# First group of a fused lightning-attention and tanh-shrink kernel: whole scores, other load order, first unit by token halves

## The chip, the cores and the metric

The kernel runs on one core of one Trainium2 chip. The metric is the device time of one execution in microseconds (us); a time without a profile is the median of several runs.

## The reference

Two parts are computed, one after the other, in 32-bit floating point.

```python
# attention: q, k, v are (4 batches, 8 heads, 768 positions, 64); one decay lam per head
for b in range(nb):                      # blocks of 64 positions, in order
    intra = einsum(qb, kb) * Dmask       # Dmask[i, j] = lam ** (i - j) for i >= j, else 0
    intra = einsum(intra, vb)
    inter = einsum(qb * lam_pow, kv_state)
    out[:, :, sl] = intra + inter
    kv_state = lam_block * kv_state + einsum(kb * rev_pow, vb)
# bridge: x is (3072 tokens, 512), the heads side by side
h = x @ w_in                             # w_in (512, 2048)
y = (h - tanh(h)) @ w_out                # w_out (2048, 512)
```

The result does not depend on the length of a block; the kernel takes blocks of 128 positions.

## The kernel before, in words

The kernel works through six **groups**. A group is one block of 128 positions in all four batches, 512 tokens. Only the very beginning concerns us here: group 0, whose attention starts from an empty state, and the first **unit** of its first matrix product. A unit is 512 of the 2048 hidden columns; there are four, 0 to 3.

**Loads.** `load_natural(g, b, names)` loads q, k or v of one batch, 256 KB each, in runs of 256 bytes. In group 0 the loads are spread over the queues of three engines: SP, ACT and POOL (GpSimd). k and v come in three DMAs: four heads whole, and the other four with the two halves of the positions exchanged. `load_weights` and `load_block` load a block of w_in (128 rows of one unit, 512 KB, in runs of 2 KB, because the input is 64 bits wide) into one of four buffers `raw64`. Block 0 goes over POOL's queue, blocks 1 to 15 over SP's. `ready["may"]` limits how many blocks may be loaded. A dictionary `begin` makes the next DMA of an engine wait for a given instruction; `tied` and `keep_in_program_order` fix the order of instructions on an engine.

**Rounding.** `weights(n)` turns loaded blocks into usable weights with `round_block`: three ScalarE (ACT) instructions (L320 to L322) and two VectorE (DVE) instructions (L324, L325).

**Attention of one batch ("chunk").** `att_transpose`: eight TensorE (PE) transposes, four of q and four of k, each four copied by ACT (L369). `att_scores`: 16 products in six pieces of 64 positions (L387, L389), then two DVE products with a `mask` of decays (L393). `att_decay`: k times its decay, one DVE instruction (L399). `kv_products`: the new state of two batches (L408), copied by `att_state` (L415). `att_out`: the outputs of two batches, in a part over all keys for the later queries (L462) and a part over half the keys (L473), then two ACT copies into `xt` (L484). The profile shows every 32-bit product as two records; a transpose is one.

**The mask.** Eight DVE scans (L110) make the decays into `whole`; a copy and a sum (L113, L114) make the six-piece `mask` of it.

**First unit.** `up_plain(0, order)` yields after each of its 16 steps. A step (i, c) is one block i of w_in times one of four outputs: c = 11 and 21 are the two halves of the unit's columns for the tokens of batches 0 and 1, c = 12 and 22 for batches 2 and 3. Every step is two products (L847), and each output is finished by tanh (L852) and a DVE difference (L853). `idle_products(n)` are n products nobody reads (L344).

The order on PE in group 0 is written out by hand: chunk 0 and chunk 1 up to the scores; the state of batches 0, 1; the transposes of chunk 2; the outputs of batches 0, 1; scores 2; transposes 3; one step of unit 0; scores 3; one step; state and outputs of batches 2, 3; then the 14 other steps. The steps take blocks 0 and 1 for all tokens first and blocks 2 and 3 after that.

Behind unit 0 come units 1 to 3 in the same way, with group 1's attention between them (`powers` is called once among them, before group 1 first needs decays), and then the second product and the other groups.

Of the kernel before, what the change touches and what calls it, by code (L numbers as in the profile page):

```python
# [18 lines left out]
BLK = 128  # L19
# [5 lines left out]
def kernel(  # L25
# [81 lines left out]
    for j in range(2):  # L107
        for p in range(NP):
            h = 2 * p + j
            nc.vector.tensor_tensor_scan(out=whole[:, j, p, :], data0=lam_all[:, h:h + 1].to_broadcast([128, BLK]),  # L110
                                         data1=ident if p < 2 else wide[:, HALF:HALF + BLK], initial=0.0, op0=AL.mult,
                                         op1=AL.add)
    nc.vector.tensor_copy(mask[:, :, 2:6, :], whole[:, :, :, HALF:BLK])  # L113
    nc.vector.tensor_tensor(mask[:, :, 0:2, :], whole[:, :, 0:2, 0:HALF], whole[:, :, 2:4, 0:HALF], op=AL.add)  # L114
# [12 lines left out]
    bwd = mask.rearrange("s j p i -> s p j i")[:, 2:6, :, HALF - 1:HALF].to_broadcast([128, NP, 2, D])  # L127

    def tied(yes, op):
        return tc.keep_in_program_order(op) if yes else op  # L130
# [12 lines left out]
    def load_natural(g, b, names):  # L143
        for name, src, bufs in (("q", q, 2), ("k", k, 3), ("v", v, 4)):
            if name in names:
                if (g, b, name) in ((0, 2, "q"), (0, 3, "q"), (0, 3, "k")):
                    x = opool.tile([128, H, D], F32, name=f"{name}_nat", tag="o")
                else:
                    x = (qpool if name == "q" else io).tile([128, H, D], F32, name=f"{name}_nat", tag=name, bufs=bufs)
                rows = src[b, :, ts(g, BLK), :].rearrange("h s d -> s h d")  # L150
                if name == "q":
                    parts = [(nc.sync, x, rows)]
                else:
                    eng = nc.sync if g > 0 else nc.scalar if b == 0 else nc.gpsimd
                    whole_ = {(0, 1, "k"): nc.scalar, (0, 2, "k"): nc.gpsimd}.get((g, b, name), nc.sync)
                    parts = [(eng, x[ts(1 - t, HALF), 4:8], rows[ts(t, HALF), 4:8]) for t in range(2)]
                    parts.insert(2 * (whole_ is nc.gpsimd), (whole_, x[:, 0:4], rows[:, 0:4]))
# [72 lines left out]
    def load_block(eng, dst, kind, n, m, first=False):  # L230

        if kind == "out":
            tied(first, eng.dma_start(out=dst, in_=moe_w_out[ts(m * KH + n, 128), :].rearrange("k (a n) -> k a n", a=2)))
        elif m < 2:
            op = tied(first, eng.dma_start(out=dst, in_=w_in_u[ts(m, 128), :, ts(n, 256)]))
            if begin.get(eng) is not None:
                wait_for(op, begin.pop(eng))
        else:
            for j in range(2):
                tied(first, eng.dma_start(out=dst[ts(1 - j, 64)], in_=w_in_u[ts(2 * m + j, 64), :, ts(n, 256)]))  # L240

    def load_weights(n):

        while ready["loaded"] < min(n, ready["may"]):
            if moe_w_in.dtype != F32:
                raw64 = stage.tile([128, 2, 256], I64, name="raw64", tag="raw64", bufs=WAHEAD)
                block = blocks[ready["loaded"]]
                load_block(nc.gpsimd if ready["loaded"] in (0, *range(NU * KI, NU * KI + 4)) else nc.sync, raw64, *block, True)
                wraw[ready["loaded"]] = raw64
            ready["loaded"] += 1  # L250

    def weights(n):

        while ready["done"] < min(n, len(blocks)):
            at_ = ready["done"]
            load_weights(at_ + WAHEAD)
            kind, n_, m = blocks[at_]
            if kind == "out" and m == 0:
                pair[n_] = pair_tiles(n_)
            w = w1[n_][:, m] if kind == "in" else pair[n_][m][:, 0:2]  # L260
            if at_ in wraw:
                round_block(w, wraw.pop(at_), at_ < 2 * KI)
            else:
                load_block(nc.gpsimd, w, kind, n_, m)
            ready["done"] += 1
# [110 lines left out]
    def att_scores(g, bs):  # L376
        for b in bs:
            qt, kt, _ = tr[g, b]

            sp = [bank("sp", "att", 4)[:, 0:6 * HALF].rearrange("s (x i) -> s x i", x=6) for _ in range(2)]  # L380
            for p in (0, 2, 1, 3):
# [14 lines left out]

    def att_decay(g, b):
        kp = raw[g, b]["k"].rearrange("s (p j) d -> s p j d", j=2)
        return tied(g != 1, nc.vector.tensor_tensor(kp, kp, bwd, op=AL.mult))  # L399

    def kv_products(g, bs):

        kv = bank("kv", *(("yb", 1) if g >= GB else ("att", 4))).rearrange("d (b p e) -> d b p e", b=2, p=NP)
# [9 lines left out]
    def att_state(g, bs):  # L413
        kv = kv_products(g, bs)
        tied(True, nc.scalar.activation(state[:, bs[0]:bs[0] + 2], kv, AF.Copy))  # L415

    reads = {}
# [24 lines left out]
    def att_out(g, bs):  # L442
# [15 lines left out]
        for n, b in enumerate(bs):  # L458
            ss, vn = sc[g, b], raw[g, b]["v"]
            for p in range(NP):  # L460
                for j in range(2):
                    tied(g == 0, nc.tensor.matmul(out=dst(n, p, j)[:, HALF:BLK], lhsT=vn[:, 2 * p + j, :],  # L462
                                                  rhs=ss[:, j, 2 + p, :], start=g == 0 and n == 0 and p % 2 == 0,
                                                  stop=n == 1 and p % 2 == 1, skip_group_check=True))
        if g < GB:
            kv = kv_products(g, bs) if g > 0 else None
# [443 lines left out]
            next(it)  # L910


    for b in (0, 1):
        att_transpose(0, (b,))
        idle_products(2 + b)
        op = att_decay(0, b)
        att_scores(0, (b,))
        if b == 0:
            idle_products(2)
    begin.update({nc.sync: op, nc.gpsimd: op})  # L920
    for b, names in ((3, "qk"), (2, "v"), (3, "v")):
        load_natural(0, b, names)
    att_state(0, (0, 1))
    att_transpose(0, (2,))

    def one_more(op):
        begin[nc.sync] = op
        ready["may"] = ready["loaded"] + 1
        load_weights(len(blocks))

    one_more(att_out(0, (0, 1)))
    unit = up_plain(0, [(2 * n + i, c + 10 * a) for n in range(KI // 2) for c in (11, 12) for i in range(2) for a in range(2)])
    att_decay(0, 2)
    att_scores(0, (2,))
    weights(1)
    idle_products(2)
    att_transpose(0, (3,))
    idle_products(5)
    one_more(att_decay(0, 3))
    steps(unit, 1)  # L940
    one_more(att_scores(0, (3,)))
    ready["may"] = len(blocks)
    steps(unit, 1)
    weights(2)
    att_state(0, (2, 3))
    att_out(0, (2, 3))
    idle_products(2)
    weights(3)
    steps(unit, 6)
    weights(4)  # L950
    steps(unit, 4)
    weights(6)
    every(unit)
    weights(2 * KI)
# [177 lines left out]
```

## Time and profile before

| | us |
|---|---|
| median of 3 runs | 655.33 (653.83 to 655.36) |
| the profiled execution | 656.1 |
| its span, first to last instruction | 654.3 |
| PE busy in the span | 646.3 (99%) |
| DVE / ACT / POOL busy | 468.9 / 244.0 / 208.8 |
| mean granted TensorE clock | 0.997 |

The span is 1.8 us shorter than the profiled execution's own time, and that execution took 0.8 us more than the median. Views are told in us from the start of the span. In the lines of the profile, "PEld" is the load of PE's weights, an "x32" counts records, and `out<-in` names what is written and read.

### The profile page before, as it was taken

Reading aid. Unit: us, or ns where it says so; the run is one execution under the profiler, and the core shown is the slowest. Engines: PE = TensorE matmul, PEld = TensorE weight load, DVE = VectorE, ACT = ScalarE, POOL = GpSimd, SP = SyncE. Lnnn points to the kernel's source line nnn. Section 1 sums busy time; section 2 is a strip of 40 time slices with the busy share of each in tenths; the row PEclk is TensorE's granted clock in tenths of the full one; section 3 lists DMA queues with packets and bytes.
Section 4 is the critical chain, followed back from the end, with each engine's and each line's share of the span. In section 5 each row is a group of like instructions: output and inputs, shape, how many; then the busy total and the mean of one; then the engine's idle time right before and its main releaser. Section 6 shows DMA issues by size and latency. Waiting matters only on the chain.

```text
span 654.3 us, 15111 instructions
## 1 busy us (share of the span) xinstructions
PE 646.3 (99%) x5888; PEld 593.3 (91%) x5888; DVE 468.9 (72%) x889; ACT 244.0 (37%) x485; POOL 208.8 (32%) x362
## 2 busy tenths in 40 slices
PE   8899999999999999999999999999999999999998
PEld 7788888888888999988999988999988899998897
DVE  4357888968878895678786668788468687466663
ACT  3676865622321222532223442213453213263210
POOL 6000135766133335202335302243401164410241
PEclk9899999999999999999999999999999999999999
DMA  9759976997769768957657956476967476721374
GB/s 196 192 168 199 260 236 216 386 276 211 172 135 224 226 183 253 212 103 184 199 178 222 246 123 167 139 241 203 232 130 160 111 265 222 223 66 35 87 246 165
DMA packets 156951, 125.80 MB, mean 192 GB/s; under 512 B 127744, under 2 KB 130048, under 8 KB 156880
## 3 DMA queue, kind: packets, MB, share of 16 engines
q0 software_dynamic: 27168, 87.91, 43.2%
q1 hardware_dynamic: 128096, 36.53, 26.4%
q8 instruction: 47, 0.77, 0.5%
q10 hardware_dynamic: 1616, 0.39, 0.4%
q14 instruction: 24, 0.20, 0.1%
HBM read 103.81 MB, written 20.97 MB: 191 GB/s over the span
## 4 chain that ended last, share of the span: by engine, by line
PE 93%; DVE 3%; DMA 2%; ACT 1%; issue 1%; ACTq 0%; DVEq 0%
PE y L553 17%; PE y L791 13%; PE zw L791 10%; PE h L847 8%; PE y L637 7%; PE z L553 6%; PE w L738 5%; PE y L738 5%; PE acc L877 4%; PE z L637 3%; PE op L462 2%; PE sp L387 2%; PE w L637 2%; PE kv L408 1%; PE op L433 1%; PE op L473 1%
## 5 line engine op out<-in xcount | busy, mean ns | idle before, releaser
L696 POOL DMA_DIRECT2D wb<-fine x148 | 79.7, 539 | 186.0 <-PE y L738 68.4
L795 ACT ACTIVATE q<-y 128x128 f32<-128x128 f32 x96 | 26.6, 277 | 142.3 <-PE y L791 141.4
L791 PE MATMUL y<-wb,g 128*128 128x128 f32 x456 | 60.2, 277 | 0.0
L847 PE MATMUL h<-xt,w 128*128 128x256 f32 x256 | 57.8, 382 | 0.4 <-DVE w L325 0.4
L791 PEld LDWEIGHTS y<-wb,g 128*128 128x128 f32 x456 | 55.1, 192 | 0.6
L847 PEld LDWEIGHTS h<-xt,w 128*128 128x128 f32 x256 | 47.6, 190 | 7.8 <-DVE w L325 1.0
L699 POOL DMA_DIRECT2D wb<-factors x44 | 23.7, 541 | 83.1 <-PE y L738 50.8
L561 ACT ACTIVATE th<-g 128x512 f32<-128x512 f32 x40 | 25.2, 630 | 66.5 <-DVE g L579 50.7
L553 PE MATMUL y<-xt,w 128*128 128x256 f32 x192 | 45.0, 379 | 0.0
L562 DVE TENSOR_TENSOR g<-g,th 128x512 f32<-128x512 f32 x40 | 27.6, 690 | 20.7 <-ACT th L561 20.7
L553 PEld LDWEIGHTS y<-xt,w 128*128 128x128 f32 x192 | 36.4, 190 | 5.1 <-ACT g L570 0.2
L791 PE MATMUL zw<-wb,g 128*128 128x128 f32 x304 | 40.3, 275 | 0.0
L393 DVE TENSOR_TENSOR ss<-sp,mask 128x384 f32<-128x384 f32 x48 | 23.7, 549 | 20.4 <-PE sp L389 20.4
L553 PE MATMUL y<-tt,ws 128*128 128x256 f32 x160 | 37.8, 379 | 0.0
L553 PE MATMUL y<-tt,w 128*128 128x256 f32 x160 | 37.8, 379 | 0.0
L553 PE MATMUL z<-xt,ws 128*128 128x256 f32 x160 | 37.8, 379 | 0.0
L738 PE MATMUL y<-wb,g 128*128 128x256 f32 x160 | 37.3, 379 | 0.0
L791 PEld LDWEIGHTS zw<-wb,g 128*128 128x128 f32 x304 | 37.0, 192 | 0.2 <-DVE g L797 0.2
L738 PE MATMUL w<-wb,g 128*128 128x256 f32 x160 | 35.3, 379 | 0.0
L553 PEld LDWEIGHTS z<-xt,ws 128*128 128x128 f32 x160 | 30.4, 190 | 4.1
L738 PEld LDWEIGHTS w<-wb,g 128*128 128x128 f32 x160 | 30.4, 190 | 4.1
L738 PEld LDWEIGHTS y<-wb,g 128*128 128x128 f32 x160 | 30.4, 190 | 4.1
(206 smaller groups left out, 1475.0 us busy)
## 6 DMA issues: line engine op xcount, KB each, us to landing
wb<-fine POOLq DMA_DIRECT2D x148, 256.0 KB, 3.5
wb<-factors POOLq DMA_DIRECT2D x44, 256.0 KB, 4.4
wb<-fine_in POOLq DMA_DIRECT2D x36, 256.0 KB, 4.1
raw<-in_moe_w_out_dram SPq DMA_DIRECT2D x12, 512.0 KB, 5.9
rest<-fine POOLq DMA_DIRECT2D x20, 256.0 KB, 4.8
raw<-in_moe_w_in_dram SPq DMA_DIRECT2D x16, 256.0 KB, 6.3
fine<-f POOLq DMA_DIRECT2D x16, 256.0 KB, 5.1
q_blk<-in_q_dram SPq DMA_DIRECT2D x128, 32.0 KB, 2.8
```

The lines of the kernel that those rows point to most:

```text
L393: op = tied(g != 1, nc.vector.tensor_tensor(ss[:, j], sp[j], mask[:, j], op=AL.mult))
L553: nc.tensor.matmul(out=t[:, m, :], lhsT=wt[:, kt, ts(m, 128)], rhs=x[:, kt, :], start=first and m == 0 and kt == 0, stop=kt == 1, skip_gro ...
L561: nc.scalar.activation(th, src, AF.Tanh)
L562: nc.vector.tensor_tensor(dst(c), src, th, op=AL.subtract)
L637: nc.tensor.matmul(out=dst[:, ts(u, 128)], lhsT=a, rhs=b, start=x in (1, 2, 5) and u == 0, stop=True, skip_group_check=True)
L696: nc.gpsimd.dma_start(out=t.rearrange("p m c -> p (m c)"), in_=fine[TWICE.index(n_), SUB.index(x_)].rearrange("p u c -> p (u c)"))
L699: nc.gpsimd.dma_start(out=t, in_=factors[XAT[FACT[n_][1]]][:, 2 * x_:2 * x_ + 2, :])
L738: nc.tensor.matmul(out=t[:, m, :], lhsT=a[:, u, kt, ts(m, 128)], rhs=wb[:, kt, :], start=first and u == 0 and m == 0 and kt == 0, stop=u = ...
L791: tied(x == STEPS[-1], nc.tensor.matmul(out=dst, lhsT=a[:, u, :], rhs=wb[:, ts(u, 128)], start=x in (1, 2) and u == 0, stop=u == NU - 1, s ...
L795: nc.scalar.activation(keep, dst, AF.Copy)
L847: tied(u == 0, nc.tensor.matmul(out=hm[c][:, m, :], lhsT=w1[u][:, i, a, ts(m, 128)], rhs=xt[0, t][:, i, :], start=m == 0 and i == 0, stop= ...
L877: nc.tensor.matmul(out=acc[n][:, r, :], lhsT=a[:, ts(r, 128)], rhs=b, start=kt == 0 and r == 0, stop=kt == KH - 1, skip_group_check=True)
```

## The change

All of it lies in group 0 and unit 0, but for one piece of DVE work that is moved into `powers`.

- k and v of group 0 come in one DMA each, positions in order: k of batches 0 and 1 on ACT's queue, the other k and all v on POOL's. Scores of group 0 are eight whole products of 128 keys by 128 queries per chunk, multiplied by `whole`; outputs are eight whole products (`first_out`, `first_tokens`).
- All w_in blocks go over SP's queue. Blocks 0 and 1 are asked for right behind q of batch 1; q2 and k2 are held until the scores of chunk 0 are multiplied, block 2 until those of chunk 1 are, and q3, k3, v2, block 3 and v3 until the first copy of the tokens of batches 0 and 1.
- The outputs of batches 0 and 1 no longer wait for chunk 2: chunks 0 and 1 are finished first, then two steps of unit 0 follow, and the parts of chunks 2 and 3 stand between further pairs of steps. The steps run by token halves: all four blocks for batches 0, 1, then all four for batches 2, 3.
- The states are copied later; kv of batches 0, 1 waits in another PSUM bank.
- The scans all use `ident`; four scans and the two instructions of `mask` (and a copy) are made in `masks`, called in `powers`.

```diff
-    nc.vector.tensor_copy(wide[:, 128:192], wide[:, 0:64])
...
+    scans(range(NP), ident)
+    def masks():
+        pin = tc.keep_in_program_order
+        pin(nc.vector.tensor_copy(wide[:, 128:192], wide[:, 0:64]))
+        scans((2, 3), wide[:, HALF:HALF + BLK])
+        pin(nc.vector.tensor_copy(mask[:, :, 2:6, :], whole[:, :, :, HALF:BLK]))
+        pin(nc.vector.tensor_tensor(mask[:, :, 0:2, :], whole[:, :, 0:2, 0:HALF], whole[:, :, 2:4, 0:HALF], op=AL.add))
     def powers():
+        masks()
...
                     parts = [(nc.sync, x, rows)]
+                elif g == 0:
+                    parts = [(nc.scalar if name == "k" and b < 2 else nc.gpsimd, x, rows)]
...
-    for b, names in ((0, "qk"), (1, "qk"), (0, "v"), (1, "v"), (2, "qk")):
-        load_natural(0, b, names)
+    for b in (0, 1):
+        load_natural(0, b, "qk")
+    ready["may"] = 1
     load_weights(1)
+    for b in (0, 1):
+        load_natural(0, b, "v")
+    ready["may"] = 2
+    load_weights(2)
...
+            if g == 0:
+                sp = [bank("sp", "att", 4).rearrange("s (p i) -> s p i", p=NP) for _ in range(2)]
+                for p in range(NP):
+                    for j in range(2):
+                        tied(True, nc.tensor.matmul(out=sp[j][:, p, :], lhsT=kt[ts(j, 64), p, :],
+                                                    rhs=qt[ts(j, 64), p, :], start=True, stop=True))
...
+                for j in range(2):
+                    op = tied(True, nc.vector.tensor_tensor(ss[:, j], sp[j], whole[:, j], op=AL.mult))
...
+    def first_out(b):
+        n, half = b % 2, b // 2
...
+        for p in range(NP):
+            for j in range(2):
+                tied(True, nc.tensor.matmul(out=out_dst(ops, n, p, j), lhsT=vn[:, 2 * p + j, :], rhs=ss[:, j, p, :],
...
+    def first_tokens(half):
+        xt[0, half] = xpool.tile([128, KI, HB], F32, name=f"xt{half}", tag=f"xt{half}")
+        ops = reads.pop((0, half))
+        return [tied(True, nc.scalar.activation(
+            xt[0, half][:, 2 * x:2 * x + 2, :].rearrange("d p (b s) -> d p b s", b=2), ops[x], AF.Copy))
+            for x in range(2)]
...
+    att_transpose(0, (0,))
+    idle_products(3)
+    held(att_scores(0, (0,)), nc.sync, nc.gpsimd)
+    load_natural(0, 2, "qk")
+    att_decay(0, 0)
+    att_transpose(0, (1,))
+    idle_products(2)
+    first_out(0)
+    att_decay(0, 1)
+    held(att_scores(0, (1,)), nc.sync)
+    more_raw(3)
+    kv = kv_products(0, (0, 1))
+    idle_products(2)
+    weights(1)
+    first_out(1)
+    held(first_tokens(0)[0], nc.sync, nc.gpsimd)
+    load_natural(0, 3, "qk")
+    load_natural(0, 2, "v")
+    more_raw(4)
+    load_natural(0, 3, "v")
+    ready["may"] = len(blocks)
+    idle_products(6)
+    unit = up_plain(0, [(i, c + 10 * a) for c in (11, 12) for i in range(KI) for a in range(2)])
+    steps(unit, 2)
+    weights(2)
+    idle_products(4)
     att_transpose(0, (2,))
-    unit = up_plain(0, [(2 * n + i, c + 10 * a) for n in range(KI // 2) for c in (11, 12) for i in range(2) for a in range(2)])
...
+    steps(unit, 2)
+    weights(3)
+    att_scores(0, (2,))
     att_decay(0, 2)
+    idle_products(6)
     att_transpose(0, (3,))
+    steps(unit, 2)
     weights(4)
+    att_scores(0, (3,))
+    first_out(2)
+    att_decay(0, 3)
+    idle_products(4)
+    first_out(3)
+    first_tokens(1)
+    first_state((0, 1), kv)
+    steps(unit, 2)
+    weights(5)
     steps(unit, 4)
+    first_state((2, 3), kv_products(0, (2, 3)))
     weights(6)
     every(unit)
```

More of the change, by code (lines that the diff above doesn't have):

```diff
@@ L106, with scans @@
         "s (j p i) -> s j p i", j=2, p=NP)
[L107 to L114, printed above, removed]
+    def scans(ps, ones):
+        for j in range(2):
+            for p in ps:
+                h = 2 * p + j
+                tc.keep_in_program_order(nc.vector.tensor_tensor_scan(
+                    out=whole[:, j, p, :], data0=lam_all[:, h:h + 1].to_broadcast([128, BLK]), data1=ones, initial=0.0,
+                    op0=AL.mult, op1=AL.add))
+    scans(range(NP), ident)
[5 more added lines that the diff above has]
+        pin(nc.vector.tensor_tensor(mask[:, :, 0:2, :], whole[:, :, 0:2, 0:HALF], whole[:, :, 2:4, 0:HALF], op=AL.add))
     def powers():
+        masks()
         for j in range(2):
@@ L127 @@
     bwd = mask.rearrange("s j p i -> s p j i")[:, 2:6, :, HALF - 1:HALF].to_broadcast([128, NP, 2, D])
+    bwd_first = whole.rearrange("s j p i -> s p j i")[:, :, :, BLK - 1:BLK].to_broadcast([128, NP, 2, D])
     def tied(yes, op):
@@ L152, in load_natural @@
                     parts = [(nc.sync, x, rows)]
-                else:
[L154 to L157, printed above, removed]
+                elif g == 0:
+                    parts = [(nc.scalar if name == "k" and b < 2 else nc.gpsimd, x, rows)]
+                else:
+                    parts = [(nc.sync, x[ts(1 - t, HALF), 4:8], rows[ts(t, HALF), 4:8]) for t in range(2)]
+                    parts.insert(0, (nc.sync, x[:, 0:4], rows[:, 0:4]))
                 for eng, to, of in parts:
@@ L239, in load_block @@
             for j in range(2):
-                tied(first, eng.dma_start(out=dst[ts(1 - j, 64)], in_=w_in_u[ts(2 * m + j, 64), :, ts(n, 256)]))
+                op = tied(first, eng.dma_start(out=dst[ts(1 - j, 64)], in_=w_in_u[ts(2 * m + j, 64), :, ts(n, 256)]))
+                if begin.get(eng) is not None:
+                    wait_for(op, begin.pop(eng))
     def load_weights(n):
@@ L247, in load_weights @@
                 block = blocks[ready["loaded"]]
-                load_block(nc.gpsimd if ready["loaded"] in (0, *range(NU * KI, NU * KI + 4)) else nc.sync, raw64, *block, True)
+                load_block(nc.gpsimd if ready["loaded"] in range(NU * KI, NU * KI + 4) else nc.sync, raw64, *block, True)
                 wraw[ready["loaded"]] = raw64
@@ L261, in weights @@
             if at_ in wraw:
-                round_block(w, wraw.pop(at_), at_ < 2 * KI)
+                round_block(w, wraw.pop(at_), at_ < 3 * KI)
             else:
@@ L378, in att_scores @@
             qt, kt, _ = tr[g, b]
+            if g == 0:
[4 more added lines that the diff above has]
+                                                    rhs=qt[ts(j, 64), p, :], start=True, stop=True))
+                if b % 2 == 0:
+                    sc[0, "half"] = wst.tile([128, 8, 256], F32, name="ss", tag="w").rearrange(
+                        "s (b j x) c -> s b j (x c)", b=2, j=2).rearrange("s b j (p i) -> s b j p i", p=NP)
+                ss = sc[0, "half"][:, b % 2]
+                for j in range(2):
+                    op = tied(True, nc.vector.tensor_tensor(ss[:, j], sp[j], whole[:, j], op=AL.mult))
+                sc[g, b] = ss
+                continue
             sp = [bank("sp", "att", 4)[:, 0:6 * HALF].rearrange("s (x i) -> s x i", x=6) for _ in range(2)]
@@ L398, in att_decay @@
         kp = raw[g, b]["k"].rearrange("s (p j) d -> s p j d", j=2)
-        return tied(g != 1, nc.vector.tensor_tensor(kp, kp, bwd, op=AL.mult))
+        return tied(g != 1, nc.vector.tensor_tensor(kp, kp, bwd if g > 0 else bwd_first, op=AL.mult))
     def kv_products(g, bs):
-        kv = bank("kv", *(("yb", 1) if g >= GB else ("att", 4))).rearrange("d (b p e) -> d b p e", b=2, p=NP)
+        kv = bank("kv", *(("yb", 1) if g >= GB else ("z", 1) if (g, bs) == (0, (0, 1)) else ("att", 4))).rearrange("d (b p e) -> d b p e", b=2, p=NP)
         for n, b in enumerate(bs):
@@ L411, in kv_products, with first_state @@
         return kv
-    def att_state(g, bs):
-        kv = kv_products(g, bs)
+    def first_out(b):
+        n, half = b % 2, b // 2
+        if n == 0:
+            reads[0, half] = [bank("op", "att", 4).rearrange("d (p b s) -> d p b s", p=2, b=2) for _ in range(2)]
+        ops, ss, vn = reads[0, half], sc.pop((0, b)), raw[0, b]["v"]
+        for p in range(NP):
+            for j in range(2):
+                tied(True, nc.tensor.matmul(out=out_dst(ops, n, p, j), lhsT=vn[:, 2 * p + j, :], rhs=ss[:, j, p, :],
+                                            start=n == 0 and p % 2 == 0, stop=n == 1 and p % 2 == 1,
+                                            skip_group_check=True))
+    def first_tokens(half):
[4 more added lines that the diff above has]
+            for x in range(2)]
+    def first_state(bs, kv):
         tied(True, nc.scalar.activation(state[:, bs[0]:bs[0] + 2], kv, AF.Copy))
@@ L462, in att_out @@
                     tied(g == 0, nc.tensor.matmul(out=dst(n, p, j)[:, HALF:BLK], lhsT=vn[:, 2 * p + j, :],
-                                                  rhs=ss[:, j, 2 + p, :], start=g == 0 and n == 0 and p % 2 == 0,
+                                                  rhs=ss[:, j, 2 + p, :], start=False,
                                                   stop=n == 1 and p % 2 == 1, skip_group_check=True))
@@ L910, in steps @@
             next(it)
[L913 to L923, printed above, removed]
-    att_transpose(0, (2,))
[L926 to L929, printed above, removed]
@@ L931, with held, more_raw @@
-    one_more(att_out(0, (0, 1)))
-    unit = up_plain(0, [(2 * n + i, c + 10 * a) for n in range(KI // 2) for c in (11, 12) for i in range(2) for a in range(2)])
+    def held(op, *engines):
+        begin.clear()
+        begin.update({eng: op for eng in engines})
+    def more_raw(n):
+        ready["may"] = n
+        load_weights(n)
+    att_transpose(0, (0,))
[4 more added lines that the diff above has]
+    att_transpose(0, (1,))
@@ L933 @@
+    steps(unit, 2)
+    weights(2)
+    idle_products(4)
+    att_transpose(0, (2,))
+    steps(unit, 2)
+    weights(3)
+    att_scores(0, (2,))
     att_decay(0, 2)
-    att_scores(0, (2,))
-    weights(1)
-    idle_products(2)
+    idle_products(6)
     att_transpose(0, (3,))
[L938 to L946, printed above, removed]
@@ L947 @@
-    idle_products(2)
-    weights(3)
-    steps(unit, 6)
-    weights(4)
+    steps(unit, 2)
+    weights(4)
+    att_scores(0, (3,))
[7 more added lines that the diff above has]
+    weights(5)
     steps(unit, 4)
+    first_state((2, 3), kv_products(0, (2, 3)))
     weights(6)
```

## The prediction, made blind

> **What bounds the kernel now.** I read the page first. PE is busy 99% of the span, so a change pays only through PE's useless time: waits, idle products, half clock.
>
> ```profile
> PE 646.3 (99%) x5888; PEld 593.3 (91%) x5888; DVE 468.9 (72%) x889; ACT 244.0 (37%) x485; POOL 208.8 (32%) x362
> ```
>
> Then the stretches of 5 us (busy PE, PEld, DVE, ACT, POOL, then clock, DMA share, GB/s). The clock drops in two of them, and DMA is saturated (about 210 GB/s) until 25 us, then half idle.
>
> ```profile
> 15.00:20.00 5.00, 3.33 (x92) 2.87 (x87) 1.26 (x4) 3.21 (x6) 0.00 (x0) 0.89 1.11 210
> 20.00:25.00 5.00, 5.00 (x57) 4.54 (x55) 1.78 (x4) 3.07 (x5) 0.00 (x0) 0.77 1.00 224
> 25.00:30.00 5.00, 5.00 (x108) 4.40 (x109) 2.05 (x4) 1.95 (x5) 0.00 (x0) 1.00 0.59 154
> ```
>
> Then the chain of waits. It waits for q2, stalls 1.68 us on nothing visible, then runs at half rate (eight transposes take 1.71 us instead of the 0.87 of later ones).
>
> ```profile
> 5.95 7.39 DMA q_nat<-in_q_dram
> ...
> 16.49 1.68 issue
> ...
> 20.28 1.71 PE tp L367 x8
> ...
> 23.29 0.87 PE h L847 x4
> ...
> 28.69 0.64 PE idle L344 x4
> 29.33 8.65 PE h L847 x40
> ```
>
> One step of unit 0 is four records, 0.87 us. Two steps stand before 29 us; the timeline of weight loads gives the other 14 (x56), and unit 0 ends at 41.3. What follows is PE-bound, so my sum is **when unit 0 ends**.
>
> ```profile
> 29.06 11.96 PEld L847 LDWEIGHTS h<-xt,w 128*128 128x128 f32 x56
> ```
>
> Last, the DMA view of three stretches: 8 to 12, 12 to 14.3 and 85 to 89 us. q1 is SP's queue, q0 POOL's.
>
> ```profile
> q1 hardware_dynamic: 1934, 0.48, 93.6%
> q0 software_dynamic: 119, 0.27, 34.5%
> ```
> ```profile
> q0 software_dynamic: 157, 0.55, 78.7%
> q1 hardware_dynamic: 482, 0.12, 25.7%
> ```
> ```profile
> q1 hardware_dynamic: 260, 0.87, 66.9%
> q0 software_dynamic: 90, 0.30, 18.9%
> ```
>
> With 256-byte runs on both, SP moves 1.8 times POOL's bytes. When w_in (2 KB runs) streams on POOL, SP's q and k fall to 0.12 MB in 2.3 us, 52 GB/s; with 4 KB runs on SP, POOL's 0.5 to 1 KB runs get 75. **The queue of small runs is pushed aside**, and the change sets w_in on SP against v on POOL.
>
> **The change, part by part.**
>
> *Wider work.* Scores go from 0.82 us a chunk (24.16 to 24.98) to eight products of 128 columns, two side by side: between 0.8 and 1.7 (no overlap); I take 0.9, by the kv row (32 records two at a time, 0.93). Outputs go from 0.85 a chunk (1.08 + 0.62 for two) to 0.9. Together +0.5 us. Mask products take 0.69 each, as L853 does at that width.
>
> *Idle products.* 27 instead of 16 behind the first 8, 0.22 us each (two records of 0.107): +2.4 us unless they fill waits; most do.
>
> *Mask work.* The front loses 0.85 us of DVE (L113, L114). Moved into `powers` are four scans (2.63/8 each), two copies and a sum: 2.4 us at about 60 us. Queued behind them are tanh differences, qd and the rounding of block 12. Their users come late (qd is made at 64.3, used at 73.3; block 12 is ready at 68.2, used after 74), so I cost it at nothing; without that slack it is 2.4 us.
>
> *Fewer DMAs.* k0 comes in one DMA; I put q0 and k0 near 4.8. The scans still wait for lam (5.2) and end at 7.85, so chunk 0's mask products end near 9.2, and q1, k1 (0.5 MB more, shared with v0) land near 8.2. Transposes 1 to 9.1, idle, outputs 0 to 10.4, scores 1 to 11.3: about 1 us ahead of today's kv.
>
> *v1.* kv of batches 0, 1 needs v1. On SP blocks 0 and 1 (1 MB) start near 8.2, on POOL v1 near 8.9. Bounds for POOL's share: 140 GB/s (twice SP, if packets take turns: POOL's are 0.55 MB / 157 = 3.5 KB in the second DMA stretch, SP's w_in packets 1.59 MB / 834 = 1.9 KB between 61 and 67 us), which gives v1 at 10.8; 25 GB/s (run by run), which gives 15.0, when everything ahead of it has come at 210 GB/s. I take 50, nearest the 52 row: blocks 0 and 1 end at 13.7, v1 at 13.9.
>
> *Clock.* PE then sits idle from 11.3 to 13.9. Today a 1.7 us gap was followed by 3.4 us of half clock (5 x 0.11 + 5 x 0.23 = 1.7 us lost). I charge 1.7; zero if the gap falls across two windows. The Trainium skill ("TensorE: Matmul & The Clock Gate", Part 1) has the clock halved after an idle window of about 3.4 us; the trace shows that less suffices. By the page's rule alone the 2.6 us gap would cost nothing and the sum would be 1.7 us lower.
>
> *The stall at 16.5.* A packet of instructions (queue q8) started at 15.3 there. Fewer score instructions put the same point of PE's program into chunk 3, with more than 6 us for the packet; I let the stall go. It is inside today's 41.3.
>
> *From v1 to the end.* kv to 14.8, idle, outputs 1 (half clock) to 17.0, token copy 0.6 to 17.6, idle to 19.2, steps 0, 1 to 20.9, idle, transposes 2 to 22.7, steps 2, 3 to 24.4, scores 2 to 25.3, six idle, transposes 3 to 27.5, steps 4, 5 to 29.2, scores 3 to 30.1, outputs 2 to 31.0, four idle to 31.9. Rounding keeps up: 1.95 us of ACT (29.71 to 31.68) and 0.7 of DVE per block, between the copies.
>
> *v3.* Outputs 3 need v3. q3, k3, v2, v3 are released at 17.6 and flow about 2 us later, an estimate (today q3, issued at 10.8, lands at 16.7, which holds its 256 KB and what is queued ahead). On SP, behind q3 and block 3, blocks 4, 5, 6 follow without a hold, as buffers come free. At 50 GB/s k3 lands at 24, v2 at 29, v3 between 32.4 (if block 6 runs out) and 34.5; I take 33. Then 0.9 for outputs, ten steps of 0.865 and 0.9 for kv: unit 0 ends at 33 + 10.45 = **43.45**, against 41.3: +2.1.
>
> *Unit 1.* Today PE waits 0.4 us for block 6. Round 5 now stands behind the copy of state 2, 3 on ACT, about 0.3 us later against unit 0's end: +0.3.
>
> Sum: **+2.4 us**, 656.1 to 658.5 on the profiled execution, which stands 0.8 over the median: 657.7.
>
> **Rivals.**
>
> *A: v comes early (faster).* If POOL keeps its share, v1 at 10.8 gives kv to 12.2, outputs 1 to 13.6, steps 0, 1 to 16.6, no half clock, v3 in time, unit 0 at 38.0: -3.3, +0.3 for unit 1, 652.3. It decides if v1 lands before about 12.6. For it: the 3.5 KB packets above, and DMA's slack after 25. Against it: in 8 to 12 us 1934 small packets passed 119 large ones, so turns are not packet for packet. The Trainium skill ("DMA: Bandwidth & Descriptors", Queues, rings and completion order) says a DMA engine takes turns between queues by packets; by that rule this rival holds, and the first DMA rows differ from it sixteenfold.
>
> *B: v is starved.* At 25 GB/s v1 lands at 15.0, half clock comes, k3 at 28.2, v3 near 34.6: unit 0 at 45.0, +4.0 with unit 1, 659.3. For it: SP's own 256-byte runs passed POOL's 1.8 to 1, so POOL's may do worse than 52.
>
> *C: no change.* v1 late, but no half clock, and v2, v3 in time: steps and idle products make 40.6 to 41.8: 655.3, within 2.
>
> **Numbers.** My case 0.31, A 0.31, B 0.18, C 0.20. Mine alone is 656.5 to 659. A measurement tells about 0.3%, 2 us, from no change. A reaches to 651.8, B to 660.2. A is the faster part, 0.31; C and the low edge of mine make 0.21; the rest is slower, 0.48.
>
> **What would show it.** Right: PE waits at kv (L408's line) for v, a clock under 0.9 between 15 and 20, POOL's landings of v1 after 13 and v3 after 31, the last step of unit 0 after 42. Wrong: v1 landed by 12 and the steps of unit 0 starting before 16; the 1.7 us stall returning elsewhere; mask work showing as a PE wait at 60 to 75.

## The result, and the profile after

The changed kernel takes **657.44 us** (median of 22 runs, 656.74 to 658.82), the kernel before 654.61 on the same chips (22 runs, 653.22 to 658.01): ratio **1.0040, 95% interval 1.0029 to 1.0051**. That is slower by 0.40%, 2.6 us (the two medians lie 2.8 us apart), more than the 0.3% that the prediction drew as its line. The prediction was 657.7.

The profiled execution of the changed kernel has a span of 655.7 us (execution 657.46), 1.4 more than that of before. The two do not differ by the whole 2.6 us because the profiled execution of before, at 656.1, lies 1.5 us over its own median. It held a half-clock stretch (18.9 to 22.3) that costs about that much, and most runs of before lack it: of the 62 that ran beside the experiments, 59 show a mean clock of 0.999 or 1.000 and 3 the 0.997 of the profiled one.

Engines, from the page of the changed kernel, and its stretches of 5 us (same columns as before):

```profile
PE 649.3 (99%) x5782; PEld 595.9 (91%) x5782; DVE 470.2 (72%) x893; ACT 244.3 (37%) x485; POOL 206.0 (31%) x354
```
```profile
15.00:20.00 5.00, 5.00 (x45) 4.50 (x44) 2.00 (x4) 2.93 (x5) 2.63 (x3) 1.00 0.74 176
20.00:25.00 5.00, 5.00 (x44) 4.39 (x44) 1.47 (x3) 2.94 (x5) 0.00 (x0) 1.00 1.00 203
25.00:30.00 5.00, 5.00 (x51) 4.39 (x51) 2.76 (x6) 2.92 (x5) 0.00 (x0) 1.00 1.06 299
```

PE is busy in all of it, and the clock is 1.00: neither the 1.68 us stall nor the half clock of before is there. By these two views alone the kernel should have become faster. The chain of waits shows why it did not (start, length, what):

```profile
2.44 8.79 DMA v_nat<-in_v_dram
11.36 1.09 PE op L451 x16
...
14.62 0.64 PE idle L361 x4
15.27 1.02 PE op L451 x16
16.29 1.53 PE idle L361 x12
17.83 1.73 PE h L895 x8
19.55 0.89 PE idle L361 x8
...
24.14 1.53 PE idle L361 x12
...
30.39 1.09 PE idle L361 x8
31.48 1.02 PE op L451 x16
32.51 5.38 PE h L895 x24
37.88 1.08 PE kv L439 x32
38.97 9.89 PE h L895 x44
```

v0 ends a wait at 11.36. From there PE is busy, but five times with idle products. The first steps of unit 0 (`h`) start at 17.8, outputs 3 at 31.48, and unit 0 ends at 42.45, against 41.26 before.

Where PE's time goes until unit 0 ends, summed from the matmul records of each trace (us; the 1.06 ahead of the first record stand in no column; e4, e6 and e10 are the kernel before with small edits, e1 and e5 the changed kernel with fewer idle products; all are explained below):

| | ends | idle products | waits | tp, sp, kv, op | h |
|---|---|---|---|---|---|
| before | 41.26 | 8.48 | 2.92 | 14.69 | 14.11 |
| e4 | 39.01 | 9.08 | 1.11 | 13.55 | 14.21 |
| e6 | 39.38 | 8.01 | 1.23 | 14.76 | 14.31 |
| e10 | 38.37 | 7.85 | 0.39 | 14.87 | 14.21 |
| after | 42.45 | 10.63 | 1.22 | 15.24 | 14.31 |
| e1 | 41.01 | 3.78 | 5.00 | 16.66 | 14.51 |
| e5 | 42.68 | 8.40 | 3.24 | 15.67 | 14.31 |

Against e6, which does the same wider work in the old order without a stall, the changed kernel loses 3.1 us, of which 2.6 are idle products. Behind unit 0 little changes: 613.0 us are left from there to the end before (654.3 less 41.26), 613.25 after. This rest differs between profiles (614.1 in e6, whose profiled execution, 655.37, is 2.0 us over its own median; 613.7 in e1), so a few tenths tell nothing.

### The profile page after: what moved, and what is told of

Its sections match the earlier page's. It is cut to its first block, busy times and chain, and to the rows that moved or that the text cites. A ratio compares the mean times of both kernels' runs of the same rounds, so it can differ in the third digit from the quotient of the medians.

```text
span 655.7 us, 14869 instructions
## 1 busy us (share of the span) xinstructions
PE 649.3 (99%) x5782; PEld 595.9 (91%) x5782; DVE 470.2 (72%) x893; ACT 244.3 (37%) x485; POOL 206.0 (31%) x354
## 4 chain that ended last, share of the span: by engine, by line
PE 80%; DMA 6%; issue 5%; SPq 4%; DVE 3%; POOL 1%; ACT 0%; POOLq 0%; DVEq 0%
PE y L601 14%; PE y L839 12%; PE zw L839 9%; PE h L895 7%; PE y L685 5%; PE z L601 5%; PE acc L925 4%; PE y L786 4%; PE w L786 4%; PE z L685 3%; SPq L181 2%; DMA q_blk<-in_q_dram 2%; SPq L169 2%; PE w L685 1%; PE sp L418 1%
## 5 line engine op out<-in xcount | busy, mean ns | idle before, releaser
L610 DVE TENSOR_TENSOR g<-g,th 128x512 f32<-128x512 f32 x40 | 27.6, 691 | 20.7 <-ACT th L609 20.7
L601 PEld LDWEIGHTS y<-tt,w 128*128 128x128 f32 x160 | 30.3, 190 | 4.2
```

What stands on the lines that cost most here:

```text
L601: nc.tensor.matmul(out=t[:, m, :], lhsT=wt[:, kt, ts(m, 128)], rhs=x[:, kt, :], start=first and m == 0 and kt == 0, stop=kt == 1, skip_gro ...
L610: nc.vector.tensor_tensor(dst(c), src, th, op=AL.subtract)
```

## The experiments

Theory 1: the order of the loads costs. w_in blocks stand ahead of q, k, v, so that v0 and later chunk 3 (q3, k3, v2, v3, released at 16.5 instead of 10.8) come late, and the idle products only fill the waits. Theory 2: PE simply has more to do (wider pieces, 27 instead of 16 idle products). Ratios are to the kernel before, run beside.

**1. No idle products behind the first 8** (e1).

```diff
-        for _ in range(n):
+        for _ in range(n if first else 0):
```

> The changed kernel without its 27 idle products behind the first 8. Queue theory (the prediction's: v, pushed aside by w_in on the DMA queues, sets the end of unit 0): PE waits for v and k where it now runs idle products, unit 0 still ends near 42.4 us, time within 0.5 us of the changed kernel, or 1.7 us more if the clock falls to half in the waits. Work theory (from 11.4 us on PE is never without an instruction, so the end is the sum of its instructions): up to 5.7 us of idle products go; waits for the token copy, for k3 (landed 23.8) and for the mask products of chunk 3 give back about 4; unit 0 ends near 40.9, time 1 to 2 us below the changed kernel, about 656.

Measured: 658.88 us (656.58 to 660.52), ratio 1.0074 (1.0056 to 1.0093). It is not faster; the runs scatter over 4 us, and the profiled one is the fastest of them. The clock divides them: 656.58 and 656.68 had a mean clock of 1.000, the four from 658.42 to 660.52 had 0.997. PE waits of the profiled run (what waits, for what; us in all, times, longest):

```profile
PE op L451 <- DMA v_nat<-in_v_dram: 2.1, 1, 2.1
PE tp L384 <- DMA k_nat<-in_k_dram: 0.9, 1, 0.9
PE op L451 <- DVE ss L407: 0.7, 2, 0.5
PE sp L400 <- ACT kt L386: 0.7, 1, 0.7
```

6.9 us of idle products went, 3.8 us of waits came, and the work is 1.4 us longer in the first records behind the waits. So most idle products cover waits. In this run, at full clock, unit 0 ends at 41.01, 1.4 us earlier than in the changed kernel, and near the 40.9 of the work theory; the median, with the lower clock, is near the other theory's case with half clock. The experiment does not decide between the two. It shows that about 1.4 us of the idle products cover no wait (v0 landed 0.45 us later in it), and that without them the clock is lower in four runs of six.

**2. lam ahead of k on ACT's queue** (e2). After the change lam lands at 6.99 (before 5.19) and the scans wait for it.

```diff
-    nc.gpsimd.dma_start(out=lam_all, ...)
+    nc.scalar.dma_start(out=lam_all, ...)
```

> The changed kernel with lam loaded first on ACT's queue instead of POOL's. lam landed at 7.0 us after the change and at 5.2 before it, and the eight scans, 2.6 us, wait for it. Late-lam theory: lam lands by 4.5, the scans end by 7.5, the mask products of chunk 0 by 9.8 instead of 10.9; with lam gone from POOL's queue v0 starts earlier too and lands by 10; outputs 0 start 1 to 1.5 us earlier and the time falls by as much, to about 656.2. Queue theory: v0 still lands at 11.2, pushed aside by q, k and w_in; time unchanged within 0.5 us.

Measured: 660.86 us, ratio 1.0115 (1.0088 to 1.0142). lam lands at 4.6, v0 at 10.43, but k0 only at 7.01 and k1 at 12.17, and PE waits 1.6 us for k and 0.8 for q. Unit 0 ends at 44.84. A miss as a remedy: k0 and k1, now behind lam on ACT's queue, land later (5.13 and 9.47 in the change).

**3. Blocks 0 and 1 held until chunk 0's mask products** (e3).

```diff
-    ready["may"] = 1
-    load_weights(1)
+    ready["may"] = 0
...
     held(att_scores(0, (0,)), nc.sync, nc.gpsimd)
+    more_raw(1)
     load_natural(0, 2, "qk")
+    more_raw(2)
```

> The changed kernel with w_in blocks 0 and 1 held until the mask products of chunk 0, so that v0 and v1 stand against no w_in. Queue theory: v0 and v1 land by 10 and 11 instead of 11.2 and 12.5, PE's wait for v goes, time 1 to 2 us lower. Work theory: outputs 0 still wait for the mask products (10.9 us), 0.3 us is gained there at most, and block 0 now lands near 14.5, so that its rounding pushes the token copy from 15.9 to about 16.5: time within 0.7 us, more likely above.

Measured: 661.58 us, ratio 1.012 (1.0105 to 1.0134). v0 lands at 9.5, v1 at 10.23, and nothing waits for v. But block 0 lands at 17.5, PE waits for its weights, and 3.4 us of half clock come with it. The largest of its PE waits:

```profile
PE h L892 <- DVE w L337: 2.9, 1, 2.9
```

Unit 0 ends at 46.95. What is taken from the blocks costs more than the wait for v did: this front needs v0 and the blocks nearly at once.

**4. The kernel before with four idle products ahead of transposes 2** (e4). Is the 1.68 us stall of before, whose waiter shows nothing, a fetch of instructions?

```diff
+    idle_products(4)
     att_transpose(0, (2,))
```

> The kernel before with four more idle products while PE waits for q of batch 2 (12.5 to 13.4 us). They put 16 instructions ahead of the 1.7 us stall at 16.5. Code theory (the stall is PE waiting for a packet of its program, queue q8): the gap stays at about the same time but 16 instructions earlier in the work, in the outputs of batches 0 and 1 (L463, L474 here) and not in scores 2; time the same within 0.7 us. Rival (scores 2 wait for a PSUM bank): the gap stays in scores 2.

Measured: 653.82 us, ratio 0.9999 (0.9989 to 1.0009). The stall moved with the count of instructions and shrank, as the PE waits say ("issue" is a wait for nothing visible):

```profile
PE op L473 <- issue: 0.4, 1, 0.4
```

Before, the packet of instructions (queue q8) ran from 15.35 to 16.70 and PE resumed at 18.16; here it ran from 14.06 to 15.17 and PE resumed at 16.68: 1.5 us behind the packet both times. The stall is code arriving late. Four more idle products (0.86 us) were free.

**5. The changed kernel with 16 idle products behind the first 8** (e5), the number of before: the last four places get 3, 2, 3, 1 instead of 6, 4, 6, 4.

> The changed kernel with 16 idle products behind the first 8, as many as before the change: the last four places 3, 2, 3, 1 instead of 6, 4, 6, 4. Work theory: 11 products of 0.22 us go, 2.4 us; the run without any showed waits of about 1 us at the places where these stand, so unit 0 ends 1.2 to 1.8 us earlier (near 41), and, the clock holding, the time falls by as much, to about 656. Clock theory: PE's waits here are long enough for half clock in some executions; the spread of the times widens as without any idle products (656.6 to 660.5) and the median does not fall.

Measured: 657.02 us, ratio 1.0046 (1.0032 to 1.006): no gain that shows. 2.2 us of idle products turned into 2.0 us of waits, the largest of which are:

```profile
PE op L451 <- DMA v_nat<-in_v_dram: 1.7, 1, 1.7
PE op L451 <- DVE ss L407: 1.2, 2, 1.1
```

**6. The kernel before with the wider work alone** (e6): keys in order, whole scores and outputs in group 0, mask work in `powers`; the old order of loads and pieces.

> The kernel before with one part of the change alone: keys in order, whole scores and whole outputs in group 0, and the mask work moved into powers; loads, order and idle products as before. Work theory: PE's time in scores of group 0 rises from about 3.4 to 4.4 us and in outputs from about 3.4 to 4.1, 1.5 us to 1.9 us more; the program is shorter, so the stall on code (0.5 to 1.7 us) leaves its place and may go; unit 0 ends near 40 to 40.5, against 39.1 for the kernel before with four more idle products, and the time is 0.3 to 1.5 us above before. Width-is-free theory (the prediction's 0.5 us): time at or below before, by the stall that goes.

Measured: 653.40 us, ratio 0.9993 (0.9981 to 1.0005). In total the wider pieces cost nothing in the old order; their price by itself is not shown, since the stall of before is gone here too. Experiment 5 does the same pieces with the same number of idle products and stands at 1.0046. So theory 2 is out, and what is slow is the new order of loads and pieces as a whole.

**7. The kernel before with the steps of unit 0 by token halves** (e7).

```diff
-    unit = up_plain(0, [(2 * n + i, c + 10 * a) for n in range(KI // 2) for c in (11, 12) for i in range(2) for a in range(2)])
+    unit = up_plain(0, [(i, c + 10 * a) for c in (11, 12) for i in range(KI) for a in range(2)])
...
     weights(3)
-    steps(unit, 6)
     weights(4)
+    steps(unit, 6)
```

> The kernel before with unit 0 by token halves alone (all four blocks for batches 0 and 1 first; rounding of blocks 2 and 3 in a row ahead of the six steps). Steps 3 on need blocks 2 and 3 two to four steps earlier. Work theory: PE has nothing else to do there, so it waits for the rounding of blocks 2 and 3 (L325), about 1 to 1.5 us, and the time rises by as much. Rival (order of steps is free while PE is behind): no wait, no change within 0.5 us.

Measured: 659.48 us, ratio 1.0084 (1.007 to 1.0099). PE now waits 1.4 us for weights in unit 0 (at 30.8) and 2.45 at the start of unit 1 (at 46.4), and two stalls on nothing visible (1.3 and 1.6) came with it, so this run does not price the order cleanly. What it does say is that token halves want blocks 2 and 3 early: with the loads of the old order they make PE wait.

**8. Chunk 3's loads early** (e8): on e5, q3 and k3 right behind q2 and k2, v2 and v3 right behind block 2.

```diff
     load_natural(0, 2, "qk")
+    load_natural(0, 3, "qk")
...
-    held(att_scores(0, (1,)), nc.sync)
+    held(att_scores(0, (1,)), nc.sync, nc.gpsimd)
     more_raw(3)
+    load_natural(0, 2, "v")
+    load_natural(0, 3, "v")
...
-    held(first_tokens(0)[0], nc.sync, nc.gpsimd)
-    load_natural(0, 3, "qk")
-    load_natural(0, 2, "v")
+    held(first_tokens(0)[0], nc.sync)
     more_raw(4)
-    load_natural(0, 3, "v")
```

> The changed kernel with 16 instead of 27 idle products behind the first 8, and with q3, k3 asked for right behind q2, k2, and v2, v3 right behind block 2, instead of at the first copy of the tokens of batches 0 and 1. Theory 1 (the change loses its time to the late loads; its idle products stand where PE would wait for them): k3 lands before 22 instead of 25, v3 before 26 instead of 29.6, the wait of 1.2 us ahead of outputs 3 goes, unit 0 ends 1.2 us earlier, at about 41.4, and the time falls by 1.0 to 1.4 against the kernel with 16 idle products, to about 655.8 (ratio 1.0025 to the kernel before); the wait for v0 of 1.7 us stays, since those loads are not touched. Rival 2 (PE has more work to do, loads only fill its pauses): not more than 0.3 us is gained, the wait comes back at another place. Rival 3 (more loads in flight push v1 or block 1 back): v1 lands after 14, unit 0 ends at 42.5 or later.

Measured: 662.35 us (660.11 to 663.48), ratio 1.0116 (1.0102 to 1.0131). A clear miss. k3 lands at 20.47 and v3 at 27.38, but block 2 at 24.72 instead of the 20.80 of the change, and this is the largest PE wait:

```profile
PE h L895 <- DVE w L337: 3.0, 1, 3.0
```

and half clock comes with it. Rival 3 holds in its outcome (unit 0 ends at 44.63), but the load pushed back is block 2; v1 landed at 12.49.

**9. The kernel before with chunk 3's loads held as in the change** (e9).

```diff
-    begin.update({nc.sync: op, nc.gpsimd: op})
-    for b, names in ((3, "qk"), (2, "v"), (3, "v")):
-        load_natural(0, b, names)
     att_state(0, (0, 1))
     att_transpose(0, (2,))
...
-    one_more(att_out(0, (0, 1)))
+    op = att_out(0, (0, 1))
+    begin.update({nc.sync: op, nc.gpsimd: op})
+    for b, names in ((3, "qk"), (2, "v"), (3, "v")):
+        load_natural(0, b, names)
+    one_more(op)
```

> The kernel before with one thing of the change: q3, k3, v2 and v3 are held until the copy of the tokens of batches 0 and 1 (about 16.5 instead of 10.8). Theory 1 (the late release of chunk 3's loads is what costs): k3 lands near 24, v3 near 27, PE waits 3 to 4 us in chunk 3, unit 0 ends at 42 to 43.5 and the time is 3 to 4 us above the kernel before (ratio 1.005 to 1.006). Rival 2 (the order of the loads is not what costs): ratio below 1.002.

Measured: 660.05 us, ratio 1.0075 (1.0062 to 1.0087), 5 us, more than expected. Held loads cost a wait for q3 and, with other instructions at other times, a stall on nothing visible; half clock came with the wait. Its two largest PE waits:

```profile
PE tp L367 <- DMA q_nat<-in_q_dram: 3.3, 2, 2.5
PE op L462 <- issue: 1.7, 1, 1.7
```

**10. e6 with block 1 asked for earlier** (e10): right behind chunk 3's loads instead of at the copy of the tokens. (The first number in the expectation is e6's 653.4.)

```diff
         load_natural(0, b, names)
+    ready["may"] = ready["loaded"] + 1
+    load_weights(len(blocks))
     att_state(0, (0, 1))
```

> The kernel before with whole scores and outputs in group 0, keys in order and the mask work moved (53.4 hundredths above 600 on its own), and block 1 of w_in asked for right behind the loads of chunk 3 instead of at the copy of the tokens of batches 0 and 1. The only wait after 12 us there is 0.93 us for block 1's weights at 26.3. Theory: block 1 lands near 21, that wait goes, unit 0 ends at 38.4, time about 652.5 (ratio 0.998), faster than both kernels. Rival: block 1 takes its share from v2, v3 and block 0, and chunk 3 waits instead: 653.4 to 654.

Measured: 653.88 us (652.96 to 654.71) beside 655.06 for before: ratio **0.9981 (0.9971 to 0.9992)**. The wait of 0.93 us at 26.3 is gone, and unit 0 ends at 38.37. This is the one version whose whole interval lies below the kernel before; the medians differ by 1.2 us. By the trace and the ratio the theory holds (expected 38.4 and 0.998); the time in us falls into the rival's 653.4 to 654, but the kernel before was slower beside it too (654.0 beside e6). That it gains on e6 is not shown: e6's interval (0.9981 to 1.0005) overlaps it, and the two did not run beside each other. The only wait for weights left comes after unit 0, at 42.6:

```profile
PE h L883 <- DVE w L335: 0.4, 1, 0.4
```

**11. v0 on SP's queue ahead of block 0** (e11), on e8.

```diff
-                    parts = [(nc.scalar if name == "k" and b < 2 else nc.gpsimd, x, rows)]
+                    parts = [(nc.scalar if name == "k" and b < 2 else nc.sync if (name, b) == ("v", 0) else nc.gpsimd, x, rows)]
```

(and `load_weights(1)` behind the loads of v).

> As the kernel with the loads of chunk 3 early, and v of batch 0 goes over SP's queue right behind q of batch 1, ahead of w_in blocks 0 and 1, instead of over POOL's. Theory 1 (the first wait of 1.7 us is v0, late because POOL's queue moves next to nothing between 5 and 8 us): v0 lands at about 9.5, v1 at about 10.5, PE starts the steps of unit 0 about 1.7 us earlier, at 16, and unit 0 ends near 39.7, as in the kernel before without its stall; time about 654.2 (ratio 1.000). Rival 2 (the wait moves to blocks 0 and 1 or to q2, which are now later): a wait of over 1 us for block 0 ahead of the first step, no gain.

Measured: 660.08 us, ratio 1.0084 (1.0062 to 1.0107). v0 at 10.19 and v1 at 11.30, and only 0.7 us of waits are left there, but block 2 lands at 27.63 and PE waits 5.8 us for it (the profiled run, 663.21, is the slowest of six). Built on e8 it could not answer its own question: the first wait went, and the larger one of e8 grew.

**12. v3 on SP's queue ahead of block 3** (e12), on e5, the release as in the change.

```diff
-                    parts = [(nc.scalar if name == "k" and b < 2 else nc.gpsimd, x, rows)]
+                    parts = [(nc.scalar if name == "k" and b < 2 else nc.sync if (name, b) == ("v", 3) else nc.gpsimd, x, rows)]
...
-    more_raw(4)
     load_natural(0, 3, "v")
+    more_raw(4)
```

> The changed kernel with 16 instead of 27 idle products behind the first 8, and v3 asked for over SP's queue ahead of block 3 instead of over POOL's behind v2; the release (first copy of the tokens of batches 0 and 1) is as in the change. Theory 1 (the last load of chunk 3 sets the end, since eight to ten steps and a kv come behind it): k3 and v3 land by 26, block 3 at 28.5 to 29.5 instead of 27.6, the wait of 1.2 us ahead of outputs 3 goes, unit 0 ends at about 41.4 instead of 42.7, time about 655.8 against 657.0 (ratio 1.0025 to 1.003 instead of 1.0046). Rival 2 (what is moved ahead only moves the wait to what is moved behind): PE waits about as long for the weights of block 3, at 32 to 34, and the time stays within 0.5 us of 657.0.

Measured: 659.58 us (658.19 to 661.9), ratio 1.0066 (1.0046 to 1.0086). This run breaks theory 1 in its late half. v3 lands at 24.05 instead of 29.64, k3 at 23.77 instead of 24.94, and yet outputs 3 start at 31.03, as in e5 (31.04). PE's timeline, and DVE's and ACT's (start, length, engine, line; in brackets the idle time ahead and what ended it):

```profile
26.53 1.16 PE L400 MATMUL sp<-qt,kt 64*128 64x128 f32 x16
27.62 1.09 PE L451 MATMUL op<-ss,v_nat 128*64 128x128 f32 x16
28.64 0.49 PE L361 MATMUL idle<-fwd 128*128 128x128 f32 x2
31.03 2.56 PE L451 MATMUL op<-ss,v_nat 128*64 128x128 f32 x16 [1.90 <-DVE ss L407]
```
```profile
27.68 0.69 ACT L332 ACTIVATE w<-raw 128x512 f32<-128x512 f32 x1 [2.13 <-DMA raw<-in_moe_w_in_dram]
...
28.89 0.76 ACT L334 ACTIVATE r<-raw 128x512 f16<-128x512 f32 x1
```
```profile
28.40 0.43 DVE L336 TENSOR_SCALAR w<-w 128x512 uint32<-128x512 uint32 x1 [2.97 <-ACT w L332]
29.68 0.69 DVE L337 CUSTOM_DVE_ANT_0 w<-w,r 128x1024 uint16<-128x1024 uint16 x1 [0.85 <-ACT r L334]
30.29 1.28 DVE L407 TENSOR_TENSOR ss<-sp,whole 128x512 f32<-128x512 f32 x2
```

Scores 3 are done at 27.6. Their mask products stand on DVE behind the rounding of block 3, because `weights(4)` is written ahead of `att_scores(0, (3,))`. The trace has DVE's work in the order of the program, though the mask products have their data 2.7 us before they begin: its rounding waits for ACT's, and ACT's for block 3, which lands at 27.60. So outputs 3 wait for a block that they do not use. 1.9 us of wait and half clock behind it (the outputs take 2.56 instead of 1.09) are the cost here.

**What this says of the change itself.** Its DVE shows the same order, but not the same wait (two lines of DVE, two of ACT):

```profile
29.11 0.69 DVE L337 CUSTOM_DVE_ANT_0 w<-w,r 128x1024 uint16<-128x1024 uint16 x1 [0.85 <-ACT r L334]
29.71 1.28 DVE L407 TENSOR_TENSOR ss<-sp,whole 128x512 f32<-128x512 f32 x2
```
```profile
26.64 0.59 ACT L386 ACTIVATE kt<-tp 128x512 f32<-128x512 f32 x1
27.12 0.67 ACT L332 ACTIVATE w<-raw 128x512 f32<-128x512 f32 x1
```

Block 3 lands at 26.68, and ACT begins to round it at 27.12 with no idle time, right behind the copy of `kt`: here the rounding follows ACT's copies and does not wait for the block. The mask products of chunk 3 begin 0.4 us after PE has gone on from scores 3 (29.30); behind scores 1, where DVE was free, they begin after 0.1. They end at 30.99, and the four idle products stand from 30.39 to 31.48 in any case. So in the changed kernel the order on DVE delays the mask products by about 0.3 us, and PE not at all. The same delay is 0.9 us in e1, 1.8 in e5 and 2.7 in e12, whose ACT waits for block 3 (0.42, 1.35 and 2.13 us), and there PE waits for it: 0.5, 1.1 and 1.9 us, as the longest of each. So the chain takes back part of what fewer idle products or an earlier v3 would give, as e5 and e12 show.

**Where the changed kernel falls behind.** Counting only useful records at a fixed price (those of e6: tp 0.143 us, sp 0.068, kv 0.032, op 0.059, h 0.220) gives the work done by a given time:

| us | 12 | 18 | 24 | 28 | 30 | 32 | 34 | 38 |
|---|---|---|---|---|---|---|---|---|
| e6 (old order) | 4.7 | 10.5 | 15.0 | 17.4 | 19.4 | 21.4 | 23.6 | 27.5 |
| e10 (old order) | 4.5 | 10.2 | 14.8 | 18.3 | 20.5 | 22.5 | 24.5 | 28.6 |
| after | 4.1 | 7.8 | 13.1 | 16.1 | 17.8 | 18.7 | 20.6 | 24.5 |
| e1 (no idle) | 3.6 | 8.7 | 13.7 | 17.4 | 18.3 | 20.1 | 22.1 | 26.0 |
| e5 (16 idle) | 3.4 | 7.8 | 13.1 | 16.7 | 18.1 | 18.5 | 20.3 | 24.3 |
| e12 (v3 early) | 4.0 | 8.5 | 13.4 | 17.6 | 18.1 | 18.4 | 19.2 | 23.2 |

By 18 us the changed kernel is 2.7 us behind e6. By 28 it has made up 1.4 of that (e6 waits 0.93 us there; behind e10 it is still 2.2). From 28 to 34 the two kernels of the old order do 6.2 us of work; after does 4.5, e1 4.7, e5 3.6, e12 1.6 (with half clock), and after is 3.0 us behind e6 again, by which its unit 0 ends later. In the changed kernel 1.1 us of that last stretch are the four idle products ahead of outputs 3, of which 0.6 cover the mask products. The loss up to 18 us comes with lam, v0 and the idle products there, and no run took that part away alone.

So what is shown is that the new order costs (experiments 5 and 6), and that PE spends most of the difference on idle products, of which about 1.4 us cover no wait (experiment 1). How the rest divides among lam, v0, k3 and the order on DVE stays open, and so does what a kernel with `weights(4)` behind the scores of chunk 3 would give: it was not run, with all or with fewer idle products.

## Why the prediction was right, and which of its steps failed

The total was right (657.7 against 657.44) and so was the direction. The place was right in words: PE late in unit 0, which ends at 42.45 (forecast 43.45). The way there was not the forecast case, and that the total came so close is luck: unit 0 was put 1.0 us too late, and 0.8 us were taken off because the profiled execution of before lay over its median, while that of the changed kernel (657.46) lies on its own.

- **POOL's share of DMA: wrong, and it was the term the forecast hung on.** I took 50 GB/s for v against w_in. DMA queues of the changed kernel, 8 to 11 us (packets, MB, share of the engines):

```profile
q0 software_dynamic: 139, 0.49, 57.6%
q1 hardware_dynamic: 216, 0.41, 47.7%
```

  POOL's v moved 0.49 MB in 3 us, 163 GB/s, more than SP's w_in: not pushed aside in this stretch, and above the upper bound (140) that I had kept for rival A. The Trainium skill ("DMA: Bandwidth & Descriptors", Queues, rings and completion order) has the engines take turns by packets; here 139 packets to 216 come near that, while 90 to 1416 in the same three microseconds before, and 20 to 628 in the changed kernel between 5 and 8 us, do not. In those earlier 3 us POOL's queue was pushed aside altogether (0.00 MB; over 5 to 13 us it moved 0.53 MB, 66 GB/s). v0 was late for that reason, and v1 behind it landed at 12.54, not 13.9; later k3 landed at 23.77 (forecast 24), v3 at 28.50, not 33. (By the forecast's own terms, 0.262 MB at 50 GB/s from 19.6, k3 would land at 24.8; and SP's 1 MB by 13.7 takes 190 GB/s, which with POOL's 50 is more than the 210 that it reckons with.)
- **Rival A's condition just came true (v1 at 12.54, before 12.6; with the same loads 12.81 in e1, 13.15 in e5), its time did not.** Steps 0 and 1 ended at 19.55, not 16.6: lam came at 6.99 instead of 5.2, v0 at 11.2, and the scores and outputs took 1.09 and 1.02 instead of 0.9. "v3 in time" held, and did not help. So kv ended at 14.62, where the forecast with v1 at 13.9 has 14.8.
- **Clock: wrong.** No 11.3 to 13.9 gap and no half clock in the profile; the 1.7 us charged were not paid.
- **"v3 sets the start of outputs 3": wrong, and this is the step that failed.** I had v3 land at 33, after PE's own row of pieces, which the forecast brings to 31.9. v3 landed 3.0 us before outputs 3 began (31.48), and experiment 12 shows that an earlier v3 does not start them earlier. What set them in the profile is the row itself, which from 11.36 on has no wait in it: 31.48 against the forecast 31.9, close through errors that cancel (no half clock; later lam and v0, wider pieces).
- **Idle products: "most do" fill waits is right, their price at nothing is wrong.** Taken away they turn mostly into waits (experiments 1, 5), and the median does not fall. But once v3 does not come last, those that fill nothing count: about 1.4 us in experiment 1. The changed kernel has 2.6 us more idle products than e6. The +2.4 us that I named for them and set aside is near that.
- **"Rounding keeps up": right for the changed kernel, with a gap.** I reckoned with room on ACT and DVE, and not with the order on DVE: chunk 3's mask products behind block 3's rounding. In the changed kernel that delays them by about 0.3 us, under the idle products; in e5 and e12 PE waits for it.
- **Wider work +0.5: undersized on PE, no cost seen in the time.** Scores take 4.37 (e6) instead of 3.36 (e4), outputs 3.75 (e6) instead of 3.48: +1.3 us of PE; experiment 6 shows no cost in the total.
- **The stall lets go: right.** Experiment 4 confirms that it was code, and that it depends on where the instruction count puts the boundary.
- **Mask work at nothing: right.** After unit 0 the changed kernel has one PE wait up to 80 us, 0.3 us for weights, which ends at 59.9, before the mask work starts (60.7); experiment 6 carries the same move and is not slower.
- **Unit 1, +0.3: the size fits, the wait does not.** From the end of unit 0 to the end of the span it is 0.2 us longer, no more than such rests differ between runs; the wait for weights that was to grow (0.4 us, ended at 45.8 before) is gone.

Of the signs that I named, the last step after 42 came; the wait for v came at outputs 0 (0.7 us), not at kv; the clock, v1 after 13 and v3 after 31 did not. Of the signs against it none came.

## What to carry to other kernels

When a piece of work is moved, write down the order on every in-order engine it uses, and ask what each instruction ahead of it waits for: a product that has all its data can stand behind a conversion that waits for a transfer. A PE that is busy all the time can still be waiting, if fill-in products stand where the wait would be; count useful records by time against a sister kernel to find where it falls behind. But the fill-in also hides which wait it covers: take it out in a run of its own, and read the clock of that run before its time. While a stretch is limited by its loads, moving one load forward moves another back: experiments 3, 8 and 11 each ended in a wait for a block of w_in. Experiment 10 moved a block forward and no new wait came.

## What the runs showed of the hardware

- **Half clock.** Waits of 2.9 us and more (e3, e8, e11) all came with half clock. Between 1.7 and 2.5 us it went both ways: 1.68 (before), 1.90 (e12) and 2.53 (e9) yes, 1.7 (e5), 2.1 (e1) and 2.45 (e7) no. The stretch at half clock is 3.4 us long in before, e3, e8 and e12, and 6.8 in e9 and e11. Stretches with it and without (the third number from the end is the clock):

```profile
30.00:35.00 5.00, 3.97 (x21) 3.17 (x22) 2.17 (x4) 1.68 (x3) 0.00 (x0) 0.66 0.66 161
```
```profile
10.00:15.00 5.00, 3.19 (x65) 2.93 (x66) 3.53 (x7) 2.36 (x4) 0.88 (x1) 1.00 0.85 228
```

  The first is e12, the second e1. The Trainium skill ("TensorE: Matmul & The Clock Gate", Part 1) has the clock halved after an idle window of about 3.4 us; the half-clock stretches here are one or two times that long, but shorter waits than that brought them.
- **Code can arrive late.** Six stalls of 0.4 to 1.7 us that wait for nothing visible came in before, e4, e7 (two) and e9 (two), and in all six PE resumed 1.4 to 1.5 us behind the end of a packet of instructions.
- **Early shares of a queue vary.** Between 5 and 8 us POOL's queue moved 0.00 MB in the changed kernel and 0.21 MB in e8, although both issue the same loads at nearly the same times up to there:

```profile
q0 software_dynamic: 20, 0.00, 7.2%
```
```profile
q0 software_dynamic: 86, 0.21, 38.8%
```

  v0 landed at 11.22 and 10.07, and at 12.01 in e5 with the same loads. So a landing of one profile is good to about 1 us in this stretch.
